# GEGLU feed-forward kernel: a finer first load of tokens and weights, transposes between the first products, and two weight chunks on the first token block before block two

## The chip, the cores and the metric

The kernel runs on one core of a Trainium2 chip. The time is the device time of the core in microseconds, and a kernel's figure is the median of several executions. One execution is also recorded by the hardware profiler; its page and trace are what the readings below are taken from. The engines are named as there: PE is the matrix engine (PEld its weight loads), DVE and ACT are the vector and the scalar engine, POOL and SP the other two. A small q behind an engine's name (SPq, ACTq) marks an instruction that issues a DMA from that engine's queue.

## What is computed

```python
# x: 1 x 2048 x 1024; w_gate, w_up: 1024 x 3584; w_down: 3584 x 1024; all bf16
def reference(x, w_gate, w_up, w_down):
    return (gelu_tanh(x @ w_gate) * (x @ w_up)) @ w_down
```

## The kernel before

The 2048 tokens are taken in two halves of 1024, and each half in two blocks of 512 (`TB`). The 1024 model columns are eight slices of 128, named kd (`KD` = 8). The 3584 hidden columns are seven chunks of 512 (`FG`), and each chunk is four slices of 128, named fi (`FPG` = 4). Both matrix stages want the contracted index on the partitions, so the tokens are needed transposed, as `xT`.

A half has two stages. In the first, the loops run over chunk, token block and fi; one `unit` makes a gate tile and an up tile of 128 hidden columns by 512 tokens, eight products each (one for each kd), all on PE at L190. `unit_tail` then runs Gelu on ACT (L200) and the product of gate and up on DVE (L201) into `hT`. In the second stage each row tile of 128 tokens is multiplied by `wd_sb`, two times 28 products of 512 output columns (L295; the last tile in two halves, L271), evacuated by ACT and stored.

PSUM is one pool of eight banks, shared by the transposes (`tp`), the gate and up tiles, the output tiles and the warm-up tile. The chunks' weights have two buffers (`wgu_pool`), so a chunk's load waits for the last reader of the chunk two before it. The down weights are loaded once, in seven pieces of 1 MB, and stay.

The start is written out by hand. ACT's queue issues the first weight piece, gate and up for kd 0 and 1 (`load_w0_piece`, L90 and L91), and then loads the Gelu table (L96). SP's queue issues the first token block in two pieces of four kd each (`load_x0_piece`, L83), the other three weight pieces of chunk 0 with the second token piece after the first of them, then block two through a transposing DMA (L124), chunk 1 (L134, L135) and the down weights (L144). PE runs nine warm-up products on constants (L108), then the sixteen transposes of the first token piece (`transpose_x_piece`, L179), then `startup_units`: the first three fi of chunk 0 at once, in six banks, kd by kd, and the transposes of the second piece just ahead of kd=3. `evac` copies the transposed banks to `xT` in turn on DVE (L150) and ACT (L152). Manual dependencies between the groups keep PE's order; the scheduler that lays out the program keeps the rest in the order of the text as far as it is ready, and places the waits. After the third fi the ordinary `unit` loop goes on: chunk 0 block one, chunk 0 block two, chunk 1 block one, and so on.

Of the kernel before, what the change touches and what calls it, by code (L numbers as in the profile page):

```python
# [10 lines left out]
BF16 = mybir.dt.bfloat16  # L11
# [7 lines left out]
def kernel(  # L19
# [8 lines left out]
    nc = tc.nc  # L28
    P = 128
    x2 = x.flatten_outer_dims()  # L30
    out2 = out.flatten_outer_dims()
    S, D = x2.shape
    F = w_gate.shape[1]
    KD = D // P
# [9 lines left out]
    NDN = D // DN  # L44
    NTS = SH // P
    TSB = TB // P
    XQ = min(512, D)
    NXQ = D // XQ
    KPQ = XQ // P
    WKP = 2 if KD % 2 == 0 else 1  # L50
    NWP = KD // WKP
    NSU = min(3, FPG)
    NWARM = 9

    xv = x2.rearrange("t (ko ki) -> t ko ki", ki=P)
    wgv = w_gate.rearrange("(ko ki) f -> ki ko f", ki=P)
    wuv = w_up.rearrange("(ko ki) f -> ki ko f", ki=P)
    wdv = w_down.rearrange("(ko ki) d -> ki ko d", ki=P)

    const_pool = ctx.enter_context(tc.tile_pool(name="const", bufs=1))  # L60
    xT_pool = ctx.enter_context(tc.tile_pool(name="xT", bufs=1))
    xs_pool = ctx.enter_context(tc.tile_pool(name="xs", bufs=1))
    hT_pool = ctx.enter_context(tc.tile_pool(name="hT", bufs=1))
    wd_pool = ctx.enter_context(tc.tile_pool(name="wd", bufs=1))
    wgu_pool = ctx.enter_context(tc.tile_pool(name="wgu", bufs=2))
    g_pool = ctx.enter_context(tc.tile_pool(name="g", bufs=3))
    o_pool = ctx.enter_context(tc.tile_pool(name="o", bufs=3))
    psum = ctx.enter_context(
        tc.tile_pool(name="psum", bufs=8, space=bass.MemoryType.PSUM)
# [2 lines left out]
    def ps_tile(name):  # L72
        return psum.tile([P, TB], F32, name=name, tag="ps")

    wd_sb = wd_pool.tile([P, KF, D], BF16, name="wd_sb")

    xs0 = xs_pool.tile([P, TSB, D], BF16, name="xs")
    xT = xT_pool.tile([P, KD, SH], BF16, name="xT")
    wg0 = wgu_pool.tile([P, KD, FG], BF16, name="wg_sb")
    wu0 = wgu_pool.tile([P, KD, FG], BF16, name="wu_sb")  # L80

    def load_x0_piece(q, eng):
        eng.dma_start(  # L83
            out=xs0[:, :, q * XQ : (q + 1) * XQ],
            in_=x2[0:TB, q * XQ : (q + 1) * XQ].rearrange("(ts p) d -> p ts d", p=P),
        )

    def load_w0_piece(wp, eng):
        k0, k1 = wp * WKP, (wp + 1) * WKP
        eng.dma_start(out=wg0[:, k0:k1, :], in_=wgv[:, k0:k1, 0:FG])  # L90
        eng.dma_start(out=wu0[:, k0:k1, :], in_=wuv[:, k0:k1, 0:FG])  # L91

    load_x0_piece(0, nc.sync)
    load_w0_piece(0, nc.scalar)

    nc.scalar.preload_act_table(ACT.Gelu_apprx_tanh)  # L96

    ident = const_pool.tile([P, P], BF16, name="ident")
    make_identity(nc, ident[:])

    warm_insts = []
    if NWARM > 0:
        warm_l = nc.const_aps.tensor(1.0, [P, P], BF16)
        warm_r = nc.const_aps.tensor(1.0, [P, TB], BF16)
        warm_ps = ps_tile("warm_ps")
        for i in range(NWARM):
            warm_insts.append(
                nc.tensor.matmul(  # L108
                    warm_ps[:], lhsT=warm_l, rhs=warm_r, start=True, stop=True
                )  # L110
            )

    x_after = {}
    for q in range(1, NXQ):
        wq = min(max((q * KPQ) // WKP - 1, 0), NWP - 1)
        x_after.setdefault(wq, []).append(q)
    for q in x_after.get(0, []):
        load_x0_piece(q, nc.sync)
    for wp in range(1, NWP):
        load_w0_piece(wp, nc.sync)  # L120
        for q in x_after.get(wp, []):
            load_x0_piece(q, nc.sync)
    for tb in range(1, NTB):
        nc.sync.dma_start_transpose(  # L124
            out=xT[:, :, tb * TB : (tb + 1) * TB],
            in_=xv[tb * TB : (tb + 1) * TB, :, :],
        )

    chunk_tiles = {0: (wg0, wu0)}

    def load_chunk(fg):
        wg_sb = wgu_pool.tile([P, KD, FG], BF16, name="wg_sb")
        wu_sb = wgu_pool.tile([P, KD, FG], BF16, name="wu_sb")
        nc.sync.dma_start(out=wg_sb[:], in_=wgv[:, :, fg * FG : (fg + 1) * FG])  # L134
        nc.sync.dma_start(out=wu_sb[:], in_=wuv[:, :, fg * FG : (fg + 1) * FG])  # L135
        return wg_sb, wu_sb

    if NFG > 1:
        chunk_tiles[1] = load_chunk(1)

    WDP = 4
    for k0 in range(0, KF, WDP):
        k1 = min(KF, k0 + WDP)
        nc.sync.dma_start(out=wd_sb[:, k0:k1, :], in_=wdv[:, k0:k1, :])  # L144

    evac_ctr = [0]

    def evac(dst, src):
        if evac_ctr[0] % 2 == 0:
            nc.vector.tensor_copy(out=dst, in_=src)  # L150
        else:
            nc.scalar.copy(out=dst, in_=src)  # L152
        evac_ctr[0] += 1

    def transpose_x_piece(q):
        kds = list(range(q * KPQ, (q + 1) * KPQ))
        banks = []
        if q == 0:
            if TSB % 2 == 0:
                banks.append(([kds[0]], (0, TSB // 2)))  # L160
                banks.append(([kds[0]], (TSB // 2, TSB)))
            else:
                banks.append(([kds[0]], (0, TSB)))
            rest = kds[1:]
            if rest:
                banks.append(([rest[0]], (0, TSB)))
                rest = rest[1:]
        else:
            rest = kds
        for i in range(0, len(rest), 2):  # L170
            banks.append((rest[i : i + 2], (0, TSB)))
        pe_insts = []
        for kd_list, (ts0, ts1) in banks:
            n = (ts1 - ts0) * P
            tp = psum.tile([P, len(kd_list), n], BF16, name="tp", tag="ps")
            for j, kd in enumerate(kd_list):
                for ts in range(ts0, ts1):
                    pe_insts.append(
                        nc.tensor.transpose(  # L179
                            tp[:, j, (ts - ts0) * P : (ts - ts0 + 1) * P],  # L180
                            xs0[:, ts, kd * P : (kd + 1) * P],
                            ident[:],
                        )
                    )
            k0 = kd_list[0]
            evac(xT[:, k0 : k0 + len(kd_list), ts0 * P : ts1 * P], tp[:])
        return pe_insts

    def mm_gu(ps, w_sb, xT_, fi, tb, kd):
        return nc.tensor.matmul(  # L190
            ps[:],
            lhsT=w_sb[:, kd, fi * P : (fi + 1) * P],
            rhs=xT_[:, kd, tb * TB : (tb + 1) * TB],
            start=(kd == 0),
            stop=(kd == KD - 1),
        )

    def unit_tail(hT, gate_ps, up_ps, fc, tb):
        g_sb = g_pool.tile([P, TB], F32, name="g_sb")
        nc.scalar.activation(out=g_sb[:], in_=gate_ps[:], func=ACT.Gelu_apprx_tanh)  # L200
        nc.vector.tensor_tensor(  # L201
            out=hT[:, fc, tb * TB : (tb + 1) * TB],
            in0=g_sb[:],
            in1=up_ps[:],
            op=ALU.mult,
        )

    def unit(hT, xT_, wg_sb, wu_sb, fi, fc, tb):
        gate_ps = ps_tile("gate_ps")
        up_ps = ps_tile("up_ps")  # L210
        for kd in range(KD):
            mm_gu(gate_ps, wg_sb, xT_, fi, tb, kd)
        for kd in range(KD):
            mm_gu(up_ps, wu_sb, xT_, fi, tb, kd)
        unit_tail(hT, gate_ps, up_ps, fc, tb)

    def startup_units(hT, wg_sb, wu_sb):
        groups = [transpose_x_piece(0)]
        su_ps = [(ps_tile("gate_ps"), ps_tile("up_ps")) for _ in range(NSU)]
        for kd in range(KD):  # L220
            for q in range(1, NXQ):
                if kd == q * KPQ - 1:
                    groups.append(transpose_x_piece(q))
            g = [mm_gu(su_ps[u][0], wg_sb, xT, u, 0, kd) for u in range(NSU)]
            g += [mm_gu(su_ps[u][1], wu_sb, xT, u, 0, kd) for u in range(NSU)]
            groups.append(g)
        if warm_insts:
            groups.insert(0, warm_insts)
        for ga, gb in zip(groups[:-1], groups[1:]):
            tc.add_manual_dep(  # L230
                gb[0].ins, ga[-1].ins.name, SCHED_DEP, reason="startup PE order"
            )
        for u in range(NSU):
            unit_tail(hT, su_ps[u][0], su_ps[u][1], u, 0)

    for h in range(NH):
        if h > 0:
            xT = xT_pool.tile([P, KD, SH], BF16, name="xT")
            for tb in range(NTB):
                t0 = h * SH + tb * TB  # L240
                nc.sync.dma_start_transpose(
                    out=xT[:, :, tb * TB : (tb + 1) * TB],
                    in_=xv[t0 : t0 + TB, :, :],
                )
        hT = hT_pool.tile([P, KF, SH], BF16, name="hT")
        for fg in range(NFG):
            if h == 0 and fg in chunk_tiles:
                wg_sb, wu_sb = chunk_tiles[fg]
            else:
                wg_sb, wu_sb = load_chunk(fg)  # L250
            for tb in range(NTB):
                fi_start = 0
                if h == 0 and fg == 0 and tb == 0:
                    startup_units(hT, wg_sb, wu_sb)
                    fi_start = NSU
                for fi in range(fi_start, FPG):
                    fc = fg * FPG + fi
                    unit(hT, xT, wg_sb, wu_sb, fi, fc, tb)
        for ts in range(NTS):
            last = h == NH - 1 and ts == NTS - 1  # L260
            o_sb = o_pool.tile([P, D], BF16, name="o_sb")
# [78 lines left out]
```

## Time and profile before

| | |
|---|---|
| median of 8 executions | 593.0 us |
| lowest, highest | 592.73, 595.12 us |
| the profiled execution, its own time | 592.94 us |
| its span, first to last instruction | 590.8 us |
| PE busy | 583.4 us, 2704 recorded products |
| ACT busy, DVE busy | 88.8 us, 78.7 us |
| moved by DMA | 45.47 MB |

Five of the eight times lie between 592.73 and 593.01 and three between 594.79 and 595.12. The span is 2.1 us shorter than the execution's time; that remainder lies ahead of the first and behind the last instruction. PE's busy time is modelled at the end of each product, and some records are missing (2704 of 2757), so intervals between starts say more than durations: eight products of 512 columns take 1.73 us from start to start, 0.216 us each.

### The profile page before, as it was taken

To read this page: it belongs to the slowest core of one execution; us is meant where nothing else is said; L and a number is where in the kernel's file an instruction comes from. 1 tells how busy PE (TensorE), PEld (TensorE's weight loads), DVE (VectorE), ACT (ScalarE), POOL (GpSimd) and SP (SyncE) were. 2 spreads that over 40 slices of the span, in tenths; PEclk is the share of its full clock that TensorE was granted. 3 is DMA by queue.
4 is the path that set the end of the run, shared out by engine and by line. 5 is a ranking of instruction groups with operands and counts; after the bars stand their busy time and mean duration, and the time that the engine had idled before them with its cause. 6 is when DMAs were issued, how large, how long until landed. Compare 5 with 4: busy or idle time off the path is not lost.

```text
span 590.8 us, 6119 instructions
## 1 busy us (share of the span) xinstructions
PE 583.4 (99%) x2704; PEld 268.6 (45%) x2757; DVE 78.7 (13%) x116; ACT 88.8 (15%) x148; POOL 0.7 (0%) x6
## 2 busy tenths in 40 slices
PE   8999999999999999999999999999999999999997
PEld 4444444444444444444444444444444444444445
DVE  0211211121122100000011221121122110000000
ACT  2211112111111110101011112111111110101010
POOL 0000000000000000000000000000000000000000
PEclk9999999999999999999999999999999999999999
DMA  9991404041221480000000413214040000000001
GB/s 273 353 378 63 143 0 143 6 138 47 96 95 48 122 181 19 23 31 18 19 18 4 140 39 105 80 63 130 13 143 1 0 1 0 24 30 19 18 19 36
DMA packets 48969, 45.47 MB, mean 77 GB/s; under 512 B 13360, under 2 KB 43440, under 8 KB 48944
## 3 DMA queue, kind: packets, MB, share of 16 engines
q1 hardware_dynamic: 45952, 40.44, 22.1%
q10 hardware_dynamic: 2992, 4.65, 2.2%
q8 instruction: 21, 0.34, 0.2%
q14 instruction: 4, 0.03, 0.0%
HBM read 37.75 MB, written 4.19 MB: 71 GB/s over the span
## 4 chain that ended last, share of the span: by engine, by line
PE 98%; DMA 1%; issue 0%; ACT 0%
PE gate_ps L190 33%; PE up_ps L190 33%; PE o_ps L295 32%; PE o_ps L271 1%; DMA xs<-in_x_dram 1%; PE tp L179 0%; ACT o_sb L287 0%
## 5 line engine op out<-in xcount | busy, mean ns | idle before, releaser
L190 PE MATMUL gate_ps<-xT,wg_sb 128*128 128x512 bf16 x878 | 210.9, 379 | 1.0
L190 PE MATMUL up_ps<-xT,wu_sb 128*128 128x512 bf16 x878 | 210.9, 379 | 0.9
L295 PE MATMUL o_ps<-wd_sb,hT 128*128 128x512 bf16 x851 | 186.8, 379 | 0.9
L190 PEld LDWEIGHTS <-wu_sb 128*128 128x128 bf16 x896 | 87.6, 98 | 105.8 <-DMA wu_sb<-in_w_up_dram 0.3
L190 PEld LDWEIGHTS <-wg_sb 128*128 128x128 bf16 x896 | 87.6, 98 | 105.2
L295 PEld LDWEIGHTS <-hT 128*128 128x128 bf16 x868 | 84.9, 98 | 102.4
L201 DVE TENSOR_TENSOR hT<-g_sb,up_ps 128x512 bf16<-128x512 f32 x112 | 76.9, 688 | 403.2 <-PE up_ps L190 392.1
L200 ACT ACTIVATE g_sb<-gate_ps 128x512 f32<-128x512 f32 x112 | 66.6, 597 | 312.4 <-PE gate_ps L190 303.8
L302 ACT CAST o_sb<-o_ps 128x512 bf16<-128x512 f32 x31 | 18.1, 585 | 172.6 <-PE o_ps L295 161.7
L279 DVE CAST o_sb<-o_ps 128x256 bf16<-128x256 f32 x1 | 0.4, 425 | 93.0 <-PE o_ps L271 93.0
L271 PE MATMUL o_ps<-wd_sb,hT 128*128 128x256 bf16 x56 | 6.3, 273 | 0.0
L271 PEld LDWEIGHTS <-hT 128*128 128x128 bf16 x56 | 5.5, 98 | 0.9
L108 PE MATMUL warm_ps<-const-bfloat16-1.0 128*128 128x512 bf16 x9 | 4.0, 626 | 0.8 <-PEq L324 0.8
L152 ACT COPY xT<-tp 128x1024 bf16<-128x1024 bf16 (+1 forms) x3 | 2.4, 799 | 7.1 <-PE tp L179 7.1
L179 PE MATMUL tp<-ident,xs 128*128 128x128 bf16 x32 | 2.1, 219 | 0.9 <-DMA xs<-in_x_dram 0.9
L179 PEld LDWEIGHTS <-xs 128*128 128x128 bf16 x32 | 1.9, 98 | 2.1 <-DMA xs<-in_x_dram 1.8
L150 DVE COPY xT<-tp 128x256 bf16<-128x256 bf16 (+2 forms) x3 | 1.4, 469 | 10.4 <-PE tp L179 10.4
L108 PEld LDWEIGHTS <-const-bfloat16-1.0 128*128 128x128 bf16 x9 | 1.2, 138 | 2.7 <-issue 2.7
L96 ACT ACT_TABLE_LOAD x1 | 1.3, 1283 | 1.8 <-issue 1.8
L287 ACT CAST o_sb<-o_ps 128x256 bf16<-128x256 f32 x1 | 0.4, 372 | 5.5 <-PE o_ps L271 5.5
masks.py:199 POOL TENSOR_SCALAR_AFFINE_SELECT ident<-ident 128x128 bf16<-128x128 bf16 x1 | 0.3, 292 | 0.1
masks.py:197 POOL MEMSET ident<- 128x128 bf16 x1 | 0.2, 204 | 0.3 <-POOLq L324 0.3
(4 smaller groups left out, 0.4 us busy)
## 6 DMA issues: line engine op xcount, KB each, us to landing
wg_sb<-in_w_gate_dram SPq DMA_DIRECT2D x13, 1024.0 KB, 5.4
wu_sb<-in_w_up_dram SPq DMA_DIRECT2D x13, 1024.0 KB, 7.2
wd_sb<-in_w_down_dram SPq DMA_DIRECT2D x7, 1024.0 KB, 13.8
out_dram<-o_sb ACTq DMA_DIRECT2D x15, 256.0 KB, 2.0
xs<-in_x_dram SPq DMA_DIRECT2D x2, 512.0 KB, 6.0
wg_sb<-in_w_gate_dram SPq DMA_DIRECT2D x3, 256.0 KB, 6.3
wu_sb<-in_w_up_dram SPq DMA_DIRECT2D x3, 256.0 KB, 6.5
wg_sb<-in_w_gate_dram ACTq DMA_DIRECT2D x1, 256.0 KB, 4.6
```

Source lines behind the costliest of these rows:

```text
L96: nc.scalar.preload_act_table(ACT.Gelu_apprx_tanh)
L108: nc.tensor.matmul(warm_ps[:], lhsT=warm_l, rhs=warm_r, start=True, stop=True)
L150: nc.vector.tensor_copy(out=dst, in_=src)
L152: nc.scalar.copy(out=dst, in_=src)
L179: nc.tensor.transpose(tp[:, j, (ts - ts0) * P : (ts - ts0 + 1) * P], xs0[:, ts, kd * P : (kd + 1) * P], ident[:],)
L190: return nc.tensor.matmul(ps[:], lhsT=w_sb[:, kd, fi * P : (fi + 1) * P], rhs=xT_[:, kd, tb * TB : (tb + 1) * TB], start=(kd == 0), stop=( ...
L200: nc.scalar.activation(out=g_sb[:], in_=gate_ps[:], func=ACT.Gelu_apprx_tanh)
L201: nc.vector.tensor_tensor(out=hT[:, fc, tb * TB : (tb + 1) * TB], in0=g_sb[:], in1=up_ps[:], op=ALU.mult,)
L271: nc.tensor.matmul(o_ps[:, 0:hh], lhsT=hT[:, fc, ts * P : (ts + 1) * P], rhs=wd_sb[:, fc, cc : cc + hh], start=(fc == 0), stop=(fc == KF - 1),
L279: nc.vector.tensor_copy(out=o_sb[:, cc : cc + hh], in_=o_ps[:, 0:hh])
L295: nc.tensor.matmul(o_ps[:], lhsT=hT[:, fc, ts * P : (ts + 1) * P], rhs=wd_sb[:, fc, c0 : c0 + DN], start=(fc == 0), stop=(fc == KF - 1),)
L302: nc.scalar.copy(out=o_sb[:, c0 : c0 + DN], in_=o_ps[:])
```

## The change

Token block one comes in four pieces of two kd each instead of two of four, all four first on SP's queue. Chunk 0's weights come in five steps (kd 0, kd 1, then pairs), each a gate and an up load, all ten on ACT's queue and in front of the Gelu table load. SP then issues chunk 1, block two's transposing load and the down weights, in this order (before: block two, chunk 1, down weights).

On PE there are eight warm-ups instead of nine. The transposes are made in pairs of kd, each kd in a bank of its own: the pair 0 and 1 ahead of the products, then a pair ahead of the products of kd 1, 3 and 5. Even kd are copied by DVE and odd kd by ACT. Each of these PE instructions has a manual dependency on the one before it.

In the first half the steps go chunk 0 block one, chunk 1 block one, chunk 0 block two, chunk 1 block two; from chunk 2 on the order is as it was. The g buffers are four instead of three, and the pools for the first token block and `xT` are declared the other way round. The second half and the output stage are unchanged.

```diff
-    NWARM = 9
+    NWARM = 8
...
-    g_pool = ctx.enter_context(tc.tile_pool(name="g", bufs=3))
+    g_pool = ctx.enter_context(tc.tile_pool(name="g", bufs=4))
...
-    load_x0_piece(0, nc.sync)
-    load_w0_piece(0, nc.scalar)
+    def load_w(fg, k0, k1, eng):
+        wg_sb, wu_sb = chunks[fg]
+        c0, c1 = fg * FG, (fg + 1) * FG
+        eng.dma_start(out=wg_sb[:, k0:k1, :], in_=wgv[:, k0:k1, c0:c1])
+        eng.dma_start(out=wu_sb[:, k0:k1, :], in_=wuv[:, k0:k1, c0:c1])
...
+    for k0 in range(0, KD, 2):
+        nc.sync.dma_start(
+            out=xs0[:, :, k0 * P : (k0 + 2) * P],
+            in_=x2[0:TB, k0 * P : (k0 + 2) * P].rearrange("(ts p) d -> p ts d", p=P),
+        )
+    for k0, k1 in ((0, 1), (1, 2), (2, 4), (4, 6), (6, 8)):
+        load_w(0, k0, k1, nc.scalar)
     nc.scalar.preload_act_table(ACT.Gelu_apprx_tanh)
...
+    new_chunk(1)
+    load_w(1, 0, KD, nc.sync)
     for tb in range(1, NTB):
-        nc.sync.dma_start_transpose(
-            out=xT[:, :, tb * TB : (tb + 1) * TB],
-            in_=xv[tb * TB : (tb + 1) * TB, :, :],
-        )
+        load_xT(xT, 0, tb, 0, KD)
...
+        def after(m):
+            nonlocal last
+            tc.add_manual_dep(
+                m.ins, last.ins.name, SCHED_DEP, reason="startup PE order"
+            )
+            last = m
+
+        def transpose_pair(k0):
+            for kd in (k0, k0 + 1):
+                tp = psum.tile([P, TB], BF16, name="tp", tag="ps")
+                for ts in range(TSB):
+                    after(
+                        nc.tensor.transpose(
+                            tp[:, ts * P : (ts + 1) * P],
+                            xs0[:, ts, kd * P : (kd + 1) * P],
+                            ident[:],
+                        )
+                    )
+                if kd % 2 == 0:
+                    nc.vector.tensor_copy(out=xT[:, kd, 0:TB], in_=tp[:])
+                else:
+                    nc.scalar.copy(out=xT[:, kd, 0:TB], in_=tp[:])
+
+        transpose_pair(0)
+        pairs = [(ps_tile("gate_ps"), ps_tile("up_ps")) for _ in range(NU0)]
         for kd in range(KD):
+            if kd % 2 == 1 and kd + 1 < KD:
+                transpose_pair(kd + 1)
+            for j in range(2):
+                for fi in range(NU0):
+                    after(mm_gu(pairs[fi][j], (wg_sb, wu_sb)[j], xT, fi, 0, kd))
...
+        steps = [(fg, tb) for fg in range(NFG) for tb in range(NTB)]
+        if h == 0:
+            steps = [(0, 0), (1, 0), (0, 1), (1, 1)] + steps[2 * NTB :]
```

## The prediction, made before the changed kernel was run

> **What bounds the kernel now.** I read the head and the chain of the page first, then the start of the timeline engine by engine, then the waits of the DMA queues, then the DMA view by stretches.
>
> ```profile
> span 590.8 us, 6119 instructions
> PE 583.4 (99%) x2704; PEld 268.6 (45%) x2757; DVE 78.7 (13%) x116; ACT 88.8 (15%) x148; POOL 0.7 (0%) x6
> ...
> PE 98%; DMA 1%; issue 0%; ACT 0%
> ```
>
> The chain is PE nearly throughout, and the waits of PE hold only two entries: 0.8 us before the warm-ups and 0.9 us for the first token piece. From the first transposes at 5.69 us PE has no hole that a change of order could fill. So the change can give only what lies ahead of the first product; it can take anything.
>
> ```profile
> 0.78 4.00 PE L108 MATMUL warm_ps<-const-bfloat16-1.0 128*128 128x512 bf16 x9 [0.78 <-PEq L324]
> 5.69 1.07 PE L179 MATMUL tp<-ident,xs 128*128 128x128 bf16 x16 [0.92 <-DMA xs<-in_x_dram]
> 6.59 0.81 PE L190 MATMUL gate_ps<-xT,wg_sb 128*128 128x512 bf16 x3
> 7.24 0.81 PE L190 MATMUL up_ps<-xT,wu_sb 128*128 128x512 bf16 x3
> 7.89 0.81 PE L190 MATMUL gate_ps<-xT,wg_sb 128*128 128x512 bf16 x3
> ```
>
> Sixteen transposes take 0.90 us (5.69 to 6.59), that is 0.056 each; then slice kd=0 takes 1.30 us (three gate and three up products), and kd=1 begins at 7.89. These are the marks I compare with.
>
> ```profile
> 0.74 0.51 ACTq L90 DMA_DIRECT2D wg_sb<-in_w_gate_dram  x1
> 1.27 0.52 ACTq L91 DMA_DIRECT2D wu_sb<-in_w_up_dram  x1
> 1.82 1.28 ACT L96 ACT_TABLE_LOAD   x1 [1.82 <-issue]
> 6.12 0.37 ACT L152 COPY xT<-tp 128x256 bf16<-128x256 bf16 x1 [3.01 <-PE tp L179]
> 6.79 1.01 ACT L152 COPY xT<-tp 128x1024 bf16<-128x1024 bf16 x1 [0.30 <-PE tp L179]
> ...
> 5.39 0.37 SPq L90 DMA_DIRECT2D wg_sb<-in_w_gate_dram  x1
> 5.80 0.47 SPq L91 DMA_DIRECT2D wu_sb<-in_w_up_dram  x1
> 7.16 6.63 SPq L124 DMA_TRANSPOSE xT<-in_x_dram  x1
> ```
>
> ACT works in order: issues, table load, copies. The next fence is from the DMA queues' own waits.
>
> ```profile
> SPq L90 <- DMA wg_sb<-in_w_gate_dram: 1.0, 1, 1.0
> SPq L124 <- DMA wu_sb<-in_w_up_dram: 0.9, 1, 0.9
> ```
>
> Nothing in the data asks for these two waits: each of those loads writes fresh memory. SP's issue at 5.39 is the ninth load of the program and follows the landing of ACT's gate piece (0.74 + 4.6 = 5.34); the transposing load is the eleventh and follows ACT's up piece (1.27 + 5.9 = 7.17). I infer that at most eight loads are under way: the ninth waits for the first, the tenth for the second, and so on, and the wait stands on the engine that issues.
>
> **The change, part by part.**
>
> Warm-ups nine to eight, copies in eight halves of a bank instead of six of mixed size, one more g buffer: the same 32 transposes and the same products. Each hides under PE's products. At cost nothing.
>
> First token block in four pieces. Before, 512 KB landed at 0.74 + 4.9 = 5.64. The DMA view of 2 to 4 us gives SP's queue 0.31 MB, so a 256 KB piece alone in front is in by about 4.0; landing trailed the bytes by 0.5 to 0.8 us, so transposes start at 4.5 to 4.8, I take 4.7. But only four transposes and one DVE copy (0.42) now stand before the first product: 4.7 + 0.22 + 0.21 (transpose end to copy, 5.69+0.11 to 6.01) + 0.42 + 0.1 = 5.65. The other 24 transposes, 1.35 us, are on the path, against 16 (0.90) before. If nothing else is late the gain is 6.59 - 5.65 - 0.45 = 0.5 us; ends 0.4 and 0.7.
>
> Ten weight loads on ACT. This is what decides. ACT issues ten instead of two, and behind them in its order stand the table load and the copy of kd=1 (odd slices are copied by ACT; before, all of ACT's loads were out by 1.79). Issues one to four: 0.74, 1.27, 1.80, 2.33. With SP's four token pieces these make eight loads, the two queues taking turns. ACT's fifth waits for its first to land, and so on to its tenth, which waits for its sixth. (Were the eight counted in the order of the program text, the fifth to eighth would wait for the token pieces; the last of those lands near 8, and ACT would be about a microsecond earlier.)
>
> Landings: ACT's queue moved 0.47 - 0.31 = 0.16 MB by 4.0, so the first 128 KB lands about 4.4; 256 KB landed at 5.34 (row above). After that the SP queue is never empty (1 MB of tokens, then 2 MB of chunk 1). The view gives the whole DMA this much:
>
> ```profile
> DMA packets 1069, 1.05 MB, mean 349 GB/s; under 512 B 48, under 2 KB 1069, under 8 KB 1069
> ```
>
> Half of 349 is 175 GB/s, 1.5 us per 256 KB. Ends: 1.83 us (5.34 to 7.17, the row of before) and 0.75 us (ACT has all). With 1.5: landings 3 to 6 at 6.09, 6.84, 8.34, 9.84. So the tenth issue goes out 9.84 to 10.35, the table load ends at 11.68 (1.28), the copy of kd=1 at 12.3 (0.59, between 0.37 for 256 and 1.01 for 1024 columns). The transposes of kd=3 also wait for it: six product banks, the uncopied kd=1 and the transposes of kd=2 fill all eight. They add 0.22, so kd=1 starts on PE at 12.55 instead of 7.89: 4.66 us late, with as many transposes (16) done as in before at 7.89. From there on the work is the same. With 1.83 it is 13.5 (5.7 late), with 0.75 about 10.3 (2.4 late).
>
> The Trainium skill, DMA: Bandwidth & Descriptors, section Queues, rings and completion order, has each DMA engine take turns between the queues packet by packet. The row of before gave ACT a third of 4 to 7 us with equal packets, where that rule gives half; with the token pieces in 512-byte packets it would give ACT two thirds while they last, and by it alone the delay would be an estimated 3.5 to 4.7 us.
>
> The clock. PE would stop at about 7.2 (kd=0 ends at 6.95, then the transposes of kd=2) and stand for 5.1 us. The trace shows what a rested PE does: the warm-ups are loaded 0.43 us apart, against 0.216 for the products of later units (1.73 for eight), although the granted-clock row reads full. So the first 3.8 us ran at half speed. No row shows a stop of this length, so the cost has two ends: 0 and half of the 4.9 us between 0.78 and 5.69, 2.45. I take half of the 3.84 us of warm-ups, 1.9, the nearest row.
>
> The Trainium skill, TensorE: Matmul & The Clock Gate, Part 1, speaks against the change here: an idle window of about 3.4 us brings the half clock back, and it takes as long at work to lift it; by that alone the cost is an estimated 1.7 us.
>
> Chunk 1's first block ahead of block two. Chunk 1 is needed four units after the start instead of eight: PE would come to it at about 12.55 + 7 x 1.30 + 0.9 + 3.45 = 26. SP issues its loads when the first token pieces have landed (about 5 and 6), and 3 MB at the rates above plus ACT's share are in by about 18: 8 us of cover, and if it were gone the cost would be what is missing of the 26. Block two's transposing load stands behind them on SP, needs about 10 us and is used at 40. Chunk 2 can load only when chunk 0's second block is done. That is now one block of four units (4 x 3.45 = 13.8 us) ahead of its use instead of two, and its 2 MB at 349 GB/s take 6: 7.8 us of cover, and any shortfall beyond that would stand on PE once. The down weights are moved by little and used at 200. Cost nothing.
>
> Sum: 592.94 (the profiled execution; 0.06 under the median of 593.0) + 4.66 + 1.9 = 599.5. The early first piece drops out, because ACT's chain doesn't contain it.
>
> **The rivals.**
>
> A is the above: 595.3 (2.4 late, no slow clock) to 601.1 (5.7 and 2.45), likeliest 599.5. For it: two waits of exactly this form in before.
>
> B, not slower: the loads don't hold ACT, or not beyond their issue time. Ten issues of 0.52 end at 5.95, table load 7.25, copy 7.85, kd=1 at 8.1, that is 0.2 late: 593.2, no change. It decides from the point at which ACT is free by 5.9. For it: the trace shows the waits only on SP. Against: SP and ACT loads shared the count (SP waited for ACT's pieces).
>
> C, faster: the copies of the odd slices are placed ahead of ACT's later loads. Then the early first piece counts: 0.5 us, 592.4, and if the last slices come late for PE, up to all of it is lost again. For over 0.2% (1.2 us, about what a measurement of this kernel can tell from no change) the first piece would have to land by 4.0, when SP's queue has only just moved its bytes.
>
> That the change doesn't do what it says: the first product would not stand before 6.59; then B's or A's time, since neither contains it.
>
> **How the numbers follow.** A 0.80, B 0.12, C 0.08. Faster takes a third of C (0.03), same the rest of C and most of B (0.15), slower A and the 0.02 of B in which ACT is held past 9 (0.82). The range must hold 8 in 10: it takes A's ends, B at its lower end, and 0.9 above A for loads in thin slices that land slower than the rows of large ones: 593.0 to 602.0. A's own range is 595.3 to 601.1.
>
> **What would show it.** Right: ACT's last load near 10, its table load after it, one ACT copy at about 12, PE idle for about 5 us after the transposes of kd=2, products 0.43 apart for some us after, and the same work from there to the end. The first transposes near 4.7 show the first piece right. Wrong: an ACT copy before 8, or PE waiting on a weight load instead of the copy, or the later stretches longer than before.

## The result, and the profile after

| | before | changed |
|---|---|---|
| median | 593.05 us (44 runs) | 597.12 us (15 runs) |
| lowest, highest | 592.73, 595.12 | 595.23, 597.83 |
| profiled execution, its own time | 592.94 | 597.42 |
| its span | 590.8 | 595.5 |

The medians stand 4.1 us apart; over matched runs the ratio is 1.005, 95% interval 1.004 to 1.006, which is 3.0 us. The two differ because 19 of the 44 executions of before lie about 1.8 us above the other 25 (taken up below): they raise its mean, but hardly its median. The time lies in the predicted range and on the predicted side, but the forecast loss was 6.5 us, more than half as much again as the medians show and over twice what the ratio shows.

The head and the chain of the changed kernel's page:

```profile
span 595.5 us, 6121 instructions
PE 584.7 (98%) x2703; PEld 269.1 (45%) x2756; DVE 79.0 (13%) x117; ACT 88.8 (15%) x149; POOL 0.7 (0%) x6
...
PE up_ps L126 32%; PE gate_ps L126 32%; PE o_ps L251 31%; PE o_ps L227 1%; DMA wu_sb<-in_w_up_dram 1%; PE tp L171 0%; ACT L102 0%; ACTq L83 0%; ACTq L84 0%; ACT xT L180 0%; ACT o_sb L243 0%
```

The chain that in before began with the token piece now passes through ACT's weight loads (L83, L84), its table load (L102) and its copy (L180). PE's start in the timeline, with start, length and, in brackets, the idle time and what ended it:

```profile
4.73 0.62 PE L171 MATMUL tp<-ident,xs 128*128 128x128 bf16 x8 [0.65 <-DMA xs<-in_x_dram]
5.64 0.81 PE L126 MATMUL gate_ps<-xT,wg_sb 128*128 128x512 bf16 x3 [0.29 <-DVE xT L178]
6.29 0.81 PE L126 MATMUL up_ps<-xT,wu_sb 128*128 128x512 bf16 x3
6.94 0.39 PE L171 MATMUL tp<-ident,xs 128*128 128x128 bf16 x4
10.49 0.58 PE L171 MATMUL tp<-ident,xs 128*128 128x128 bf16 x4 [3.17 <-ACT xT L180]
10.87 1.49 PE L126 MATMUL gate_ps<-xT,wg_sb 128*128 128x512 bf16 x3
```

The first product stands at 5.64 (before 6.59), then PE stops for 3.17 us ahead of the transposes of kd=3, and kd=1 begins at 10.87 (before 7.89): 2.98 us late. ACT's order is why:

```profile
2.65 0.46 ACTq L83 DMA_DIRECT2D wg_sb<-in_w_gate_dram  x1
4.71 0.38 ACTq L84 DMA_DIRECT2D wu_sb<-in_w_up_dram  x1
...
8.05 0.48 ACTq L84 DMA_DIRECT2D wu_sb<-in_w_up_dram  x1
8.56 1.28 ACT L102 ACT_TABLE_LOAD   x1 [8.56 <-DMA wu_sb<-in_w_up_dram]
9.85 0.58 ACT L180 COPY xT<-tp 128x512 bf16<-128x512 bf16 x1
```

Ten issues of under half a microsecond each are spread over 7.8 us, then come the table and the copy. The stretch behind the stop, from the view by stretches (length, PE busy, ..., granted clock, DMA share, GB/s):

```profile
10.49:13.95 3.46, 3.46 (x12) 1.50 (x12) 0.00 (x0) 0.58 (x1) 0.00 (x0) 0.51 1.10 348
```

The clock is 0.51 for 3.46 us: 3.46 x 0.49 = 1.70 us of PE's work lost. The fourth unit begins here, in before (first line) and in the changed kernel:

```profile
17.84 1.89 PE L190 MATMUL gate_ps<-xT,wg_sb 128*128 128x512 bf16 x8
22.34 1.89 PE L126 MATMUL gate_ps<-xT,wg_sb 128*128 128x512 bf16 x8
```

The step from kd=1 is 22.34 - 10.87 = 11.47 us against 17.84 - 7.89 = 9.95 in before, 1.52 more; the rest of the 1.70 fell on the transposes ahead of kd=1. From there the two traces run parallel: the last store is issued at 592.81 against 588.32, 4.49 us later, as the fourth unit was 4.50 later. Of the 15 runs, four lie between 595.2 and 595.8 with a mean clock of 0.999 to 1.000, and eleven between 596.6 and 597.8 at 0.996 to 0.997: the clock does not fall to half in every run, and where it does the runs are 1.8 us longer (means 597.18 and 595.39).

### The profile page after: what moved, and what is told of

Read it like the earlier page. It is cut to its first block, busy times and chain, and to the rows that moved or that the text cites. A ratio compares the mean times of both kernels' runs of the same rounds, so it can differ in the third digit from the quotient of the medians.

```text
span 595.5 us, 6121 instructions
## 1 busy us (share of the span) xinstructions
PE 584.7 (98%) x2703; PEld 269.1 (45%) x2756; DVE 79.0 (13%) x117; ACT 88.8 (15%) x149; POOL 0.7 (0%) x6
## 3 DMA queue, kind: packets, MB, share of 16 engines
q10 hardware_dynamic: 4656, 6.23, 3.1%
HBM read 37.75 MB, written 4.19 MB: 70 GB/s over the span
## 4 chain that ended last, share of the span: by engine, by line
PE 97%; DMA 1%; issue 1%; ACT 0%; ACTq 0%
PE up_ps L126 32%; PE gate_ps L126 32%; PE o_ps L251 31%; PE o_ps L227 1%; DMA wu_sb<-in_w_up_dram 1%; PE tp L171 0%; ACT L102 0%; ACTq L83 0%; ACTq L84 0%; ACT xT L180 0%; ACT o_sb L243 0%
## 5 line engine op out<-in xcount | busy, mean ns | idle before, releaser
L178 DVE COPY xT<-tp 128x512 bf16<-128x512 bf16 x4 | 1.7, 425 | 17.2 <-PE tp L171 17.2
L180 ACT COPY xT<-tp 128x512 bf16<-128x512 bf16 x4 | 2.3, 585 | 7.1 <-PE tp L171 7.0
```

The lines of the kernel that those rows point to most:

```text
L178: nc.vector.tensor_copy(out=xT[:, kd, 0:TB], in_=tp[:])
L180: nc.scalar.copy(out=xT[:, kd, 0:TB], in_=tp[:])
```

## The experiments

**All copies on DVE.** Is it the copy, or would late weights hold PE as long?

```diff
-                if kd % 2 == 0:
-                    nc.vector.tensor_copy(out=xT[:, kd, 0:TB], in_=tp[:])
-                else:
-                    nc.scalar.copy(out=xT[:, kd, 0:TB], in_=tp[:])
+                nc.vector.tensor_copy(out=xT[:, kd, 0:TB], in_=tp[:])
```

> The changed kernel with all eight transposed banks copied by DVE; ACT still issues the ten weight loads, but nothing that PE waits for stands behind them. Theory: the stop of 3.2 us on the copy of kd=1 and the 3.41 us at half clock that follow it (1.7 us) both go. kd=1 starts near 7.4 us and the time falls from 597.1 to about 592.4, unless the weight slices, which land at 8.4/10.0 (kd 2-3), 12.5/14.0 (kd 4-5) and 15.5/17.0 (kd 6-7) in the changed kernel, are then late: they would cost up to 1.6 us, so 592.4 to 594.1, and the clock stays whole. Rival (late weights are the real bound, the copy only hides it): PE stops for the weights instead, above 595.5.

Measured 594.00 us, ratio to before 1.0019 (1.0011 to 1.0028); clock 1.000. kd=1 begins at 7.60. What is left is the weights:

```profile
PE up_ps L126 <- DMA wu_sb<-in_w_up_dram: 0.9, 2, 0.7
```

So the late copy, with the half clock behind its stop, is worth 3.1 us of the 4.1, and behind it stood a second, smaller lateness: the slices of kd 2 to 5 go out at 2.70 to 6.23, and their landings end two waits of 0.9 us in all. By the starts of the groups of three products PE loses 1.25 us there (8.90 to 9.91 and 12.35 to 13.89, where such a group takes 0.65). The rival falls as the main cause and stays as the remainder.

**A filler in the stop.** Fourteen products on constants between the products of kd=0 and the transposes of kd=2.

```diff
+            if kd == 1:
+                fill_ps = ps_tile("fill_ps")
+                for _ in range(14):
+                    after(
+                        nc.tensor.matmul(
+                            fill_ps[:], lhsT=warm_l, rhs=warm_r, start=True, stop=True
+                        )
+                    )
```

> The changed kernel with 14 more products on constants on PE between the products of kd=0 and the transposes of kd=2, 3.0 us of work inside the stop; everything else the same, the copy of kd=1 as late as before. Theory (the stop costs twice: its length, and the half clock after it): kd=1 still starts near 10.9, but the products after it are 0.216 us apart at once, and 1.7 us go: 595.4. Rival (the half clock comes whatever PE does in the stop, or the filler delays kd=1): 597.1 or more.

Measured 595.52 us (595.44 to 595.75), 1.6 under the changed kernel; kd=1 at 10.60. The same stretch as above:

```profile
10.49:13.95 3.46, 3.41 (x26) 1.93 (x25) 0.76 (x2) 0.70 (x2) 0.00 (x0) 1.00 1.10 347
```

26 products and transposes instead of 12, at a clock of 1.00, and all five runs have a mean clock of 0.999 or 1.000. PE's idling in the stop brings the half clock; the copy's lateness is the stop. The two terms are now priced apart.

**Six loads on ACT.** The copies as they were, the loads of kd 4 to 7 moved to SP ahead of chunk 1.

```diff
-    for k0, k1 in ((0, 1), (1, 2), (2, 4), (4, 6), (6, 8)):
+    for k0, k1 in ((0, 1), (1, 2), (2, 4)):
         load_w(0, k0, k1, nc.scalar)
+    for k0, k1 in ((4, 6), (6, 8)):
+        load_w(0, k0, k1, nc.sync)
```

> The changed kernel with the copies as they are (odd slices on ACT) and only the loads of kd 4 to 7 moved from ACT to SP, ahead of chunk 1: ACT issues six loads instead of ten. Theory (ACT's order decides: last load issued, 1.28 us of table load, 0.58 us of copy): the sixth load goes out at about 4.7, the table is loaded by 6.4, the copy of kd=1 done by 7.0, which is when PE needs it; no stop over 0.3 us, no half clock, 592.5 to 593.0. Rival (the count of ACT's loads doesn't matter, only that any loads or the table stand ahead of the copy): a stop of 2 us or more stays, 595 or more.

Measured 592.98 us (592.89 to 593.20), ratio 0.9998 (0.9989 to 1.0006). ACT's last load goes out at 4.17, the copy of kd=1 is made at 5.88, PE doesn't stop. Four issues fewer on ACT take the whole loss away, so it was their place in ACT's order. But the lead of the first product (5.32 against 6.59 in before) does not reach the end. Part of it goes ahead of kd=1, as the loads of PE's stationary operand show:

```profile
4.19 0.77 PEld L173 LDWEIGHTS <-xs 128*128 128x128 bf16 x8 [0.75 <-DMA xs<-in_x_dram]
4.91 0.15 PEld L128 LDWEIGHTS <-wg_sb 128*128 128x128 bf16 x1
5.32 0.10 PEld L128 LDWEIGHTS <-wg_sb 128*128 128x128 bf16 x1 [0.25 <-issue]
5.69 0.10 PEld L128 LDWEIGHTS <-wg_sb 128*128 128x128 bf16 x1 [0.27 <-issue]
```

Eight transposes take 0.77 us where they took 0.45 in the changed kernel, and the first gate products are 0.41 and 0.37 apart: PE begins before the clock is whole. Even so kd=1 begins at 7.21, 0.68 us ahead of before. Another 0.35 go at kd=2, where the up products wait until 9.51 (8.51 + 0.65 = 9.16 without a wait) for weights whose load is ACT's sixth, held until 4.17. At the fourth unit 0.30 us are left (17.54 against 17.84), and these go behind the last store: from its issue to the end of the span it is 2.85 us here, 2.52 in before.

**Both together**: all copies on DVE, and four loads on SP.

> As the one with all copies on DVE, and the four loads of kd 4 to 7 issued by SP ahead of chunk 1 instead of by ACT. Theory: neither the copy nor the weights are late; the first piece at 4.7 us and three more pairs of transposes between the products give 592.4 to 592.6, 0.5 us under before. Rival (the 0.5 us doesn't exist because the thin slices and 512-byte token packets slow the loads): 593.0 or more.

Measured 593.18 us, ratio 1.0002 (0.9993 to 1.0011): no difference, the expected 0.5 us is missing here too. The first gate products take 1.29 us for three (5.50) instead of 0.81, again the clock, so that kd=1 begins at 7.72, only 0.17 us ahead of before; and the end behind the last store is 2.85 us, as in the six-load variant.

**The table first.** `preload_act_table` moved ahead of ACT's loads.

> The changed kernel with the Gelu table loaded ahead of ACT's ten weight loads instead of behind them. Theory (ACT's chain is the holds of the loads, then table, then copy): the holds that end last are those for the token pieces and for ACT's early slices, which move by well under 1.3 us, so the copy of kd=1 starts about 8.5 to 9.3 instead of 9.85 and the stop shrinks from 3.2 to about 2 us; with a stop that short the clock stays whole in most runs. 593.9 to 595.5. Rival (table and issues only trade places, the chain is a sum of issue times): the copy starts at 9.85 as before and the time stays at 597.1.

Measured 596.77 us, ratio 1.0050 (1.0036 to 1.0065), above what I expected.

```profile
0.73 1.28 ACT L94 ACT_TABLE_LOAD   x1 [0.73 <-PEq L280]
0.77 0.42 ACTq L83 DMA_DIRECT2D wg_sb<-in_w_gate_dram  x1
...
5.54 0.39 ACTq L83 DMA_DIRECT2D wg_sb<-in_w_gate_dram  x1
...
8.50 0.63 ACTq L84 DMA_DIRECT2D wu_sb<-in_w_up_dram  x1
9.17 0.59 ACT L180 COPY xT<-tp 128x512 bf16<-128x512 bf16 x1 [7.16 <-issue]
```

The table load no longer counts (the loads are issued while it runs), and the copy is 0.68 earlier. But the fifth load is now held until 5.54 instead of going out at 2.65, so the weights of kd 2 and 3 come late, and PE waits 0.7 and 0.7 us for them: what the copy gives the weights take. Two of the five runs, the recorded one among them, kept a clock of 1.000 and were no faster than the three at 0.996 to 0.997, so here the half clock seems to have cost nothing beyond the late weights. The holds are the long part of ACT's chain.

**The order of the chunks alone**, put into the kernel before: chunk 1's load ahead of block two, and the steps in the new order.

```diff
...
+        steps = [(fg, tb) for fg in range(NFG) for tb in range(NTB)]
+        if h == 0:
+            steps = [(0, 0), (1, 0), (0, 1), (1, 1)] + steps[2 * NTB :]
...
```

> The kernel before with nothing changed but the order of the steps (chunk 0 block one, chunk 1 block one, chunk 0 block two, chunk 1 block two) and of SP's loads behind chunk 0 (chunk 1 ahead of block two). Theory (the reorder costs nothing: chunk 1 is in by about 17, needed at about 21; chunk 2's lead of 13.8 us covers its 6): 593.0, no wait of PE in the profile. Rival (chunk 1 or chunk 2 comes late with the shorter lead): 593.5 to 597, with PE waiting for a weight load at about 21 or 48 us.

Measured 593.13 us beside 593.19, ratio 0.9996 (0.9983 to 1.0008), and PE waits for nothing behind the first token piece. This part costs nothing, as predicted.

**The two groups of before.** In before 25 of 44 runs lie at 592.7 to 593.2 and 19 at 594.5 to 595.1, while the six-load variant has one group. Two kernels change only the number of warm-ups of before (`NWARM`).

> The kernel before with eleven warm-ups instead of nine, so that PE is busy until about 5.4 instead of 4.7 and the hole of 0.9 us ahead of the first transposes closes. Theory (the before kernel's two groups of times, 592.9 and 594.8, are runs in which the clock is whole from the first transposes and runs in which the hole ahead of them puts the full clock off by a further stretch; the six-load variant, which has no such hole, has all eleven runs between 592.9 and 593.2): the upper group goes, all runs within 592.7 to 593.6. Rival (the two groups come from elsewhere): about a third of the runs stay near 594.8.

> The kernel before with seven warm-ups instead of nine: PE's work on constants ends near 3.8 instead of 4.7 us, the hole ahead of the first transposes grows from 0.9 to 1.9 us. Theory (the hole decides how often the full clock comes late): more than half of the runs, against about a third with nine warm-ups and none with eleven, are in an upper group near 594.8, and the median moves up by 1 to 2 us. Rival (the hole has nothing to do with it): median 593.0, a third of the runs above 594.

With eleven: 593.03 us, all 11 runs between 592.78 and 593.26, beside 11 of 23 runs of before over 594; ratio 0.9989 (0.9978 to 0.9999). With seven: 594.17 us, 7 of 12 runs over 594, beside 5 of 23 of before; ratio 1.0008 (0.9995 to 1.0020), so the share moved as expected, on few runs, and the ratio is not settled. The hole ahead of the first transposes (0.34, 0.92 and 1.55 us of PE's wait in the profiles with eleven, nine and seven) goes with how often the upper group appears; clearly so for eleven. That it is the clock is likely but not shown: no run of the upper group was recorded with a profile.

**Half of the block transposed by DMA**: kd 4 to 7 loaded with one transposing DMA on SP, in the place of two token pieces and sixteen transposes.

> The six-load variant with the tokens of kd 4 to 7 of block one loaded transposed by one DMA on SP, instead of two token pieces and sixteen transposes on PE. Theory (behind the first product PE is the only bound, 16 transposes are 0.9 us of it): 592.1, 0.9 us below the six-load variant and 0.8 below before, if the transposed half is in by 11. Rival (the transposing load holds SP and its small packets slow the weight slices): PE waits for weights or tokens at about 10 to 13 and the time is 593 to 596.

Measured 597.66 us (594.9 to 599.71), ratio 1.0063 (1.0038 to 1.0087), above even the rival's 593 to 596. Its mechanism is what the trace shows: SP spends 4.30 us on issuing the transposing load, and the up weights of kd=1, issued by ACT at 2.16, land only at 11.96 (7.61 in the changed kernel) and are late for PE. That it is the transposing load's own traffic that delays them is likely, not tested by itself. Five of the six runs have a mean clock of 0.994 to 0.997, so the half clock came on top.

```profile
1.80 4.30 SPq L88 DMA_TRANSPOSE xT<-in_x_dram  x1
...
12.00 1.25 PE L129 MATMUL up_ps<-xT,wu_sb 128*128 128x512 bf16 x3 [3.62 <-DMA wu_sb<-in_w_up_dram]
```

**The weights of kd 2 and 3 early.** Five loads on ACT; SP's order is token pieces one and two, the up weights of kd 2 and 3, then the rest by kd.

```diff
...
+    load_x0(0)
+    load_x0(2)
+    load_w(0, 0, 1, nc.scalar)
+    load_w(0, 1, 2, nc.scalar)
+    load_w(0, 2, 4, nc.scalar, nc.sync)
+    load_x0(4)
+    load_w(0, 4, 6, nc.sync)
+    load_x0(6)
+    load_w(0, 6, 8, nc.sync)
...
```

> As the six-load variant, but ACT issues five loads and SP's order is token piece one, token piece two, the up weights of kd 2 and 3, token piece three, then the weights of kd 4 and 5, piece four, the weights of kd 6 and 7, chunk 1. In the six-load variant PE waits at kd=2 for these up weights, whose load goes out at 4.2 because it is the ninth; here it is the eighth and goes out at about 1.8. Theory (that load's late issue is what takes the early start back): no wait at kd=2, kd=2 begins at 8.3 to 8.6 and the time is 592.3 to 592.7. Rival (the clock takes it back: the first products run at half speed because eight warm-ups end before the full clock comes): 592.8 to 593.2 with the first eight transposes over 0.7 us.

Measured 592.87 us, ratio 0.9994 (0.9985 to 1.0003): not told from before. Six runs lie at 592.5 to 592.8 and five at 592.9 to 593.4; the five have a mean clock of 0.999, five of the six 1.000. That this is the late clock of the six-load variant is likely, not shown. The profile is that of the next run.

> The variant with the weights of kd 2 and 3 issued early once more, for its profile, since the recorded execution of the first run was throttled to 0.655 of the clock from end to end. Theory: no PE wait at kd=2. If the early start is taken back by the clock, the eight transposes and the first gate products show it (over 0.7 us for eight transposes, over 0.81 us for three products); if neither shows, kd=2 starts near 8.4 and the time is near 592.5.

One run, 592.57 us beside 592.76. PE waits for no weights, kd=1 begins at 7.04 and kd=2 at 8.34, and the last store is issued 0.85 us earlier than in before (first line):

```profile
588.32 0.34 ACTq L288 DMA_DIRECT2D out_dram<-o_sb  x1
587.47 0.34 ACTq L252 DMA_DIRECT2D out_dram<-o_sb  x1
```

Yet the span is 590.7 against 590.8. The other 0.75 us are lost behind the last store: 3.27 us to the end of the span against 2.52. In the trace SP ends the program with five waits in a row for the load and store counters; in before the last store's counter is in the last of the five, here it is in the first, and four more waits follow it. These four take 0.30 us (589.10 to 589.39). A further 0.46 us pass between two of SP's instructions behind them (589.47 to 589.93; 0.05 in before), and what that gap waits for no run shows. The other versions bear out only the smaller part: with the last store's counter in the first wait and no such gap it is 2.70 to 2.85 us to the end of the span (the changed kernel, all copies on DVE, the filler, six loads, both together, the table first), with it in the last wait 2.41 to 2.54.

**The last store on the other counter.** Chunk 2 of the first half in three pieces of each weight, four loads more, which moves the last store's counter on by four places in the row of eight.

```diff
-                load_w(fg, 0, KD, nc.sync)
+                cuts = (0, 2, 4, KD) if h == 0 and fg == 2 else (0, KD)
+                for k0, k1 in zip(cuts[:-1], cuts[1:]):
+                    load_w(fg, k0, k1, nc.sync)
```

> The variant with the weights of kd 2 and 3 issued early, and chunk 2 of the first half loaded in three pieces of each weight instead of one, four loads more at a time when the queues are idle. Only their number matters: the last store then falls on the same one of the eight counters as in the kernel before. Theory (the 0.84 us that PE is ahead of before at the last product are mostly lost behind it: from the issue of the last store to the end of the span it is 3.2 us there against 2.5 in before, because SP looks at the counters one by one and the last store's is the first it looks at): 2.5 us again, and 592.0 to 592.4. Rival (the longer end is chance, or has to do with something else at the end): 2.9 us or more, 592.5 to 592.9.

Measured 591.97 us (591.52 to 592.40) beside 593.15, ratio 0.9969 (0.9956 to 0.9981): the only version that beats both kernels clearly. The ratio holds 1.8 us, of which part is before's upper group (5 of its 14 runs; this version has none in 9): against before's lower nine it is 1.15 us (means 591.89 and 593.04). Last store in its trace:

```profile
587.74 0.34 ACTq L254 DMA_DIRECT2D out_dram<-o_sb  x1
```

The span is 590.1, so 2.4 us remain, as in before: the last store's counter is in the last wait again, and the gap of 0.46 us is gone too. The four waits (0.3 us) are thus shown to go with the counter. For the gap that is not shown: four more loads lengthen SP's program as well, and that rival was not tried.

## Why the prediction was right or wrong

*What bounds the kernel* was right as to PE. That only its start was open was not: the last version gains at the end of the program as well. *First token piece*: transposes predicted at 4.7, measured 4.73; first product 5.65 against 5.64. So close a match is partly luck: in the other versions that load the first piece first the transposes begin between 4.19 and 4.71. That a gain of 0.5 us would follow if nothing else were late was wrong by two things I had no term for: the clock is not whole until 5.7 (six-load variant), and the end of the program is longer, by 0.2 us in the changed kernel, 0.3 with four loads on SP and 0.75 with the weights of kd 2 and 3 early.

*Ten weight loads on ACT*: the mechanism was right (held issues, then the table, then the copy, then the transposes of kd=3 on the freed bank). The step that failed is the sentence that "ACT's fifth waits for its first to land, and so on to its tenth, which waits for its sixth". It put the last issue at 9.84; it went out at 8.05. In the trace every load carries one of eight completion counters, dealt to ACT and SP in one joint order, nearly that in which they issued, and five of the first eight went to ACT, not four: its fifth load went out unheld at 2.65. In the completion events of the trace token pieces one and two land at 4.68 and 5.95, ACT's third and fourth loads at 6.38 and 7.61, and its sixth to ninth loads follow at 4.71, 5.96, 6.40 and 7.63; the tenth then waits only for its turn. ACT's chain hung on the landing of 128 KB slices and token pieces that were early in the queues, and not on that of 256 KB slices that were themselves held. The rate is not what made the forecast too long: the landings that I had worked out at 175 GB/s for ACT's third, fourth and fifth loads, 6.09, 6.84 and 8.34, came later still, at 6.38, 7.61 and 8.38. Nor would four and four have saved the step. The table-first version has just that arrangement, and there, too, ACT's fifth doesn't wait for its first: its fifth, seventh and ninth loads (5.54, 6.83, 8.09) follow the landings of token pieces two, three and four (5.52, 6.81, 8.06), and the tenth goes out at 8.50. In both traces a load waits for the one that stands eight before it in the joint order of the two queues, and SP's loads take places in that order too. I even had an arrangement of this kind in a bracket, a microsecond shorter, and let it decide nothing. With the last issue at 8.05 the rest of my sum (table, copy, 0.22 us of transposes) gives 10.76 for kd=1; measured 10.87. So this term was 4.66 and measured 2.98.

*The clock*: predicted 1.9 from the length of the warm-ups, measured 1.70 in the profiled run. The nearness is partly luck, since the 3.84 us of warm-ups are set by their number, nine. The Trainium skill's window (TensorE: Matmul & The Clock Gate, Part 1), which I had only set beside it, gives an estimated 1.7 and agrees with the row of 0.51 over 3.46 us. That the stop of 3.2 us, shorter than that window, brought it in 11 of 15 runs and not in the other four is what the runs add. *The queues*: from the Trainium skill's turns packet by packet (DMA: Bandwidth & Descriptors, Queues, rings and completion order) I had worked out two thirds for ACT while the token pieces last. The trace of the changed kernel shows less: from 4 to 6 us, with work on both queues, ACT's moved 0.19 MB and SP's 0.46, under a third, as in before. Why, no run here shows.

*Chunk order, copies, down weights at cost nothing*: right. The order of the steps and of SP's loads was measured alone; warm-ups, copies and the g buffer were not, but behind the half clock the two traces run parallel. One lateness had no term in the sum: with the stop gone, the weights of kd 2 to 5 cost PE 1.25 us (all copies on DVE), because their issues are held too.

The sum by the measured terms: span 590.8 + 2.98 + 1.52 + 0.2 at the end = 595.5, which is the span measured.

Rival B, no change because ACT is free by 5.9, was the right point: with six loads ACT is free of loads at 4.6 and the time is that of before. Rival C did not come about: the first ACT copy stands behind all ten loads, at 9.85.

## What to carry to other kernels

Count what stands in an engine's order ahead of the first thing that another engine needs of it: loads issued from a computing engine are cheap only until they are held, and held loads hold the copies behind them. Before pricing such a chain, settle which earlier load each issue waits for, from the joint order of both queues' loads, since here that decided its length more than the bandwidth did. A start made earlier has to be followed to the end of the program: it can run into a half clock, into the next load, or be lost behind the last store.

## What the runs showed of the hardware that was not expected

A table load of 1.28 us on ACT doesn't keep ACT from issuing DMAs: the loads went out at 0.77 to 2.33 beside it. PE's half clock came back after a stop of 3.2 us in 11 of 15 runs, and lasted 3.46 us in the recorded one. With a hole of 0.34 us ahead of the first work no run lies in an upper group (0 of 11); with 0.92 us 19 of 44 do, about 1.8 us higher, and with 1.55 us 7 of 12. The end of the program costs 2.4 to 2.5 us from the issue of the last store when that store's counter is in the last of SP's five waits, and 2.7 to 3.3 us when it is in the first; about 0.3 us of this is the four waits behind it, and the rest of the longest is open.
